# A batch's pp·w1 from eight fp32 products in 64x32 tiles, straight into its final layout, in place of split products through DRAM

## The chip, the cores and the metric

One core of one Trainium2 chip. The metric is device time in microseconds (us) of one launch; lower is better. The kernel before has a median of 977.68 us over three runs.

## The reference

For each of 8 batches: packed attention of 8 heads (32 packed rows `p` against 576 keys, then 576 queries `q` against the 32 packed rows), and a mixer on its result.

```python
p_packed = sm_attn(p, k, v)               # (8, 8, 32, 64): pp
out = sm_attn(q, p_packed, p_packed)      # a @ pp, a: (8, 8, 576, 32)
x = out.transpose(0, 2, 1, 3).reshape(B, S, H * D)     # (8, 576, 512)
h = x.transpose(0, 2, 1) @ U @ V
u = x + h.transpose(0, 2, 1)
ch = np.maximum(u @ w_ch1, 0.0) @ w_ch2   # w_ch1 (512, 2048), w_ch2 (2048, 512)
return u + ch
```

U, V, w_ch1 (w1) and w_ch2 (w2) arrive as float64; q, k, v, p as float32. Since x is a @ pp for each head, u @ w1 is (a plus its mixing) @ (pp·w1), where pp·w1 has 256 rows (8 heads of 32) and 2048 columns for each batch. This pp·w1 of a batch is what the change is about.

## The kernel before, in words

**The work.** The 2048 columns of w1 are done in two sweeps over all 8 batches, 1024 columns in each. A sweep has 8 steps `kt` of 128 columns for a batch. `gemm1(kt)` makes h from pp·w1 (tiles `wt`, hi and lo) and the attention weights (`ah`, `al`), 24 matmuls of 288 columns; ScalarE and VectorE take it out through relu as hi and lo; `gemm2(kt-1)`, one step behind, multiplies by w2 into four accumulators `o`, 12 matmuls of 512 columns (`joint` does the rest of the rows of two batches together). Every float32 product there is three products of float32r parts (`mm3`, lines 166 to 168: hi·hi, hi·lo, lo·hi). Sweep 0 stores `o` as `sum`, sweep 1 adds it.

**Around it, in sweep 0.** The attention of later batches runs in between: `packs` (keys, values and p of batch b+2), `attention` and `mixing` (queries of batch b+1). Float64 weights are made float32 by `convert`: a load of `bits` on SP's queue (two ahead), a ScalarE Abs (L228), four VectorE instructions (L229, L230, L234, L235), then a split into hi (ScalarE, L297) and lo (GpSimd, L298). What sweep 0 needs of w1 (8 items) and of w2 (8) is converted at the start, in one chain of 16; what sweep 1 needs of w2 in batches 2 and 3, of w1 in batches 5 and 6.

**pp·w1 before.** `fold(r, parts)` does it for two batches at once. pp is split into `lwh`, `lwl` (block diagonal), and for each 512 columns `c` and pair of heads `pr` an `mm3` with w1's hi and lo goes to one PSUM bank (68 in all, 204 matmuls), ScalarE copies it to an `ev` tile (L598, 3 of them, shared with the stores of `o` and of w2), and SP stores it to `wsb` in DRAM (L600). `load_wt` brings 256 columns back in the layout that gemm1 wants (L615, one `raw` tile), `split_wt` makes hi (ScalarE, L620) and lo (GpSimd, L621). This goes on 64 times, two pieces ahead.

**What sets the order.** All engines run fixed programs. The order is set while the program is written by a planner, `Chains`: each piece of side work is a generator with a due time, its needs (`banks`, `take`) and the flags that it comes after; `place()` puts ready pieces in between the products, and `until(...)` places nothing but side work till something is done. Times in `step(...)` are the planner's estimates. An engine that waits in its program holds all that stands behind it, and SP's queue, which issues every DMA, does so too. The first gemm1 stands behind `until("attention0", "fold0_0", "w2_0")`, the third step of batch 0 behind `until("fold0_1")`, which needs the packs of batch 1. Six PSUM banks serve the side work before the first gemm1 and two (`psT`) after it.

## Time and profile before

| | us |
|---|---|
| runs | 977.68, 978.88, 975.24 |
| median | 977.68 |
| profiled execution, its own time | 974.02 |
| its span in the trace | 972.3 |
| TensorE's mean granted clock in it, as a share of 2.4 GHz | 0.925 |

Section 1 of the page gives busy times by engine: TensorE 851.4 us (88%), VectorE 412.9, ScalarE 367.6, GpSimd 198.0. TensorE's busy time counts a matmul from its start to its modelled end, so where matmuls follow one another closely their starts tell how long one takes. A granted clock of 1.00 is 2.4 GHz, of 0.50 is 1.2 GHz; a stretch in between had some of each. In rows of waits, "A <- B" means that A stood still until B was done.

### The profile page before, as it was taken

The numbers are of one execution on the slowest core, as the hardware profiler recorded it, in microseconds if no ns is written. First come the engines' busy times: TensorE is split into PE (matmuls) and PEld (weight loads), VectorE is DVE, ScalarE is ACT, GpSimd is POOL, SyncE is SP. The second block draws the span as 40 slices with busy tenths as digits, with TensorE's granted clock in tenths as the row PEclk, the third lists the DMA queues.
The fourth block names the chain that finished last, engine by engine and source line by source line (L and its number), as shares of the span: only waits on it lengthen the run. The fifth ranks groups of instructions, "written<-read, shape, count | busy, mean of one in ns | idle before, by whom it ended". The sixth has DMA issues, their size and how long they took to land.

```text
span 972.3 us, 15520 instructions
## 1 busy us (share of the span) xinstructions
PE 851.4 (88%) x5452; PEld 703.8 (72%) x5452; DVE 412.9 (42%) x1122; ACT 367.6 (38%) x1065; POOL 198.0 (20%) x193
## 2 busy tenths in 40 slices
PE   4563697888999839999987999999999999999997
PEld 2342375666678628688766878888888888898996
DVE  2663556433556624444477722314131332423232
ACT  3542454343455424445544452334333322322220
POOL 0223223111233212212234411111111111111110
PEclk9665788798999979999998999999999999999999
DMA  7535554254547652623555162674353524324131
GB/s 218 161 86 172 176 158 130 98 155 117 182 153 243 210 173 73 201 90 123 155 158 179 55 179 93 245 227 149 117 165 112 190 66 139 115 83 160 42 109 66
DMA packets 101917, 139.06 MB, mean 143 GB/s; under 512 B 18896, under 2 KB 67408, under 8 KB 101840
## 3 DMA queue, kind: packets, MB, share of 16 engines
q1 hardware_dynamic: 101840, 138.07, 45.8%
q8 instruction: 44, 0.72, 0.3%
q14 instruction: 33, 0.27, 0.1%
HBM read 87.62 MB, written 50.41 MB: 142 GB/s over the span
## 4 chain that ended last, share of the span: by engine, by line
PE 71%; DMA 9%; DVE 8%; ACT 4%; POOL 3%; issue 3%; SPq 1%; DVEq 0%; ACTq 0%; POOLq 0%
PE o L166 13%; PE o L167 13%; PE o L168 13%; PE h_ps L166 7%; PE h_ps L168 6%; PE h_ps L167 6%; DMA xt<-in_k_dram 3%; PE t_ps L378 2%; PE t_ps L167 2%; PE t_ps L395 2%; PE t_ps L168 2%; PE t_ps L166 1%; DMA wsb<-ev 1%; PE t_ps L405 1%; DVE ts L229 1%
## 5 line engine op out<-in xcount | busy, mean ns | idle before, releaser
L712 DVE SCALAR_TENSOR_TENSOR hl<-h_ps,hh 128x256 fp32r<-128x256 f32 x256 | 107.7, 421 | 326.8 <-ACT hjh L710 325.8
L166 PE MATMUL o<-w2h,hh 128*128 128x512 f32 x512 | 209.4, 409 | 8.7 <-DVE ev L734 3.8
L167 PE MATMUL o<-w2l,hh 128*128 128x512 f32 x512 | 202.7, 396 | 3.5 <-POOL w2l L298 3.5
L168 PE MATMUL o<-w2h,hl 128*128 128x512 f32 x512 | 202.6, 396 | 0.0
L710 ACT ACTIVATE hh<-h_ps 128x256 fp32r<-128x256 f32 x256 | 98.4, 386 | 265.5 <-PE h_ps L168 265.3
L166 PE MATMUL h_ps<-ah,wth 128*128 128x288 f32 x512 | 159.2, 311 | 17.1 <-ACT wth L620 13.6
L621 POOL TENSOR_TENSOR wtl<-raw,wth 128x512 fp32r<-128x512 f32 x64 | 83.8, 1310 | 428.2 <-ACT wth L620 415.9
L168 PE MATMUL h_ps<-ah,wtl 128*128 128x288 f32 x512 | 154.2, 301 | 1.2 <-POOL wtl L621 1.2
L167 PE MATMUL h_ps<-al,wth 128*128 128x288 f32 x512 | 154.0, 301 | 0.0
L166 PEld LDWEIGHTS h_ps<-ah,wth 128*128 128x128 f32 x512 | 99.4, 194 | 31.0 <-ACT wth L620 13.8
L166 PEld LDWEIGHTS o<-w2h,hh 128*128 128x128 f32 x512 | 97.3, 190 | 30.5 <-DVE ev L734 5.2
L168 PEld LDWEIGHTS o<-w2h,hl 128*128 128x128 f32 x512 | 97.2, 190 | 21.0
L167 PEld LDWEIGHTS o<-w2l,hh 128*128 128x128 f32 x512 | 97.5, 190 | 17.4 <-POOL w2l L298 4.1
L167 PEld LDWEIGHTS h_ps<-al,wth 128*128 128x128 f32 x512 | 99.6, 194 | 4.0
L168 PEld LDWEIGHTS h_ps<-ah,wtl 128*128 128x128 f32 x512 | 99.1, 194 | 1.8 <-POOL wtl L621 1.8
L598 ACT COPY ev<-t_ps 128x512 f32<-128x512 f32 x68 | 39.9, 586 | 105.5 <-PE t_ps L168 77.8
L166 PE MATMUL t_ps<-w1h,lwh 128*128 128x512 f32 x68 | 32.5, 478 | 33.6 <-ACT ev L598 17.2
L378 PE MATMUL t_ps<-ident,xt 128*128 128x128 f32 x256 | 44.5, 311 | 9.7 <-DVE aT L551 3.2
L379 ACT COPY xT<-t_ps 128x512 f32<-128x512 f32 x64 | 37.6, 590 | 36.6 <-PE t_ps L378 36.5
L710 ACT ACTIVATE hjh<-h_ps 128x32 fp32r<-128x32 f32 x256 | 50.1, 196 | 0.0
L378 PEld LDWEIGHTS t_ps<-ident,xt 128*128 128x128 f32 x256 | 36.1, 161 | 18.4 <-DVE aT L551 3.5
L229 DVE TENSOR_SCALAR ts<-ts 128x512 f32<-128x512 f32 x32 | 31.0, 970 | 37.9 <-ACT ts L228 37.7
(130 smaller groups left out, 1165.3 us busy)
## 6 DMA issues: line engine op xcount, KB each, us to landing
bits<-in_moe_w_ch_dram SPq DMA_DIRECT2D x32, 512.0 KB, 4.1
wsb<-ev SPq DMA_DIRECT2D x128, 128.0 KB, 2.4
raw<-wsb SPq DMA_DIRECT2D x64, 256.0 KB, 2.7
xt<-in_k_dram SPq DMA_DIRECT2D x16, 512.0 KB, 4.7
xt<-in_v_dram SPq DMA_DIRECT2D x16, 512.0 KB, 4.7
xt<-in_q_dram SPq DMA_DIRECT2D x16, 512.0 KB, 4.2
sum<-ev SPq DMA_DIRECT2D x32, 256.0 KB, 2.2
part<-sum SPq DMA_DIRECT2D x32, 256.0 KB, 4.6
```

What stands on the lines that cost most here:

```text
L166: nc.tensor.matmul(ps, lhsT=lh, rhs=rh, start=start, stop=False)
L167: nc.tensor.matmul(ps, lhsT=lh, rhs=rl, start=False, stop=False)
L168: nc.tensor.matmul(ps, lhsT=ll, rhs=rh, start=False, stop=stop)
L229: nc.vector.tensor_single_scalar(t, t, LEAST, op=ALU.max)
L378: nc.tensor.transpose(t_ps[:, P * a:P * a + P], pairs[:, P * c:P * c + P], ident)
L379: nc.scalar.copy(t[:, 2 * h2:2 * h2 + 2, HT:HS], t_ps.rearrange("p (h x) -> p h x", h=2))
L395: nc.tensor.matmul(ss[r][hs, :HS], lhsT=lT[rs, g, hs], rhs=t[rs, h, HT * (1 - r):HT * (1 - r) + HS], start=True, stop=True)
L405: nc.tensor.transpose(t_ps[:, o:o + P], src[:, BLOCK[kk]:BLOCK[kk] + P], ident)
L598: nc.scalar.copy(st, w_ps)
L621: nc.gpsimd.tensor_tensor(lo, raw, hi.bitcast(F32), op=ALU.subtract)
L710: nc.scalar.activation(hi, src, AF.Relu)
L712: nc.vector.scalar_tensor_tensor(lo, src, 0.0, hi.bitcast(F32), op0=ALU.max, op1=ALU.subtract)
```

## The change

For each sweep, batch and 512 columns `fold` is now a chain of its own, 32 in all. It multiplies pp by w1 with eight plain fp32 matmuls of 512 columns, each in a tile of 64 rows by 32 columns of the array (a pair of head and column group by one of two row groups), into two PSUM banks, in the layout that gemm1 reads. From there ScalarE copies hi and VectorE subtracts lo into `wt`, of which there are two of 512 columns. Nothing goes to DRAM. w1 is kept as float32 (in 3 slots of 512 columns for each of four tiles), so that its conversion ends with VectorE's last instruction; a w1 item is loaded with two DMAs of 64 rows. Each fold may start when its batch's packs are done, w1's four items for its columns are there and a `wt` is free, that is, when gemm1 has ended with the piece before the last. Step 0 and step 4 of each batch stand behind `until` for their fold. The first chain of conversions no longer comes after the loads of batch 0's keys and values, and its first two items are loaded on ScalarE's DMA queue; w1's second half is converted in two chains of four, in batches 6 and 7. `pn` has two buffers and is loaded ahead of its turn, x tiles go from 6 to 7, pp goes to DRAM once for each batch and comes back for all batches at the start of sweep 1.

```diff
-    QW = 256
+    QW = 512
     NPC = NKS * P // QW
...
-    NX = 6
+    NX = 7
...
-    wsb = {(b, c): dram.tile([H * NP, 512], F32, name=f"wsb{b}_{c}", tag=f"wsb{b}_{c}")
-           for b in range(B) for c in range(4)}
...
-    side = Chains(6, xt=NX, xT=2, e=3, eT=2, pT=1, aT0=1, aT1=1)
+    side = Chains(6, xt=NX, xT=2, e=3, eT=2, pT=1, ppT=4, aT0=1, aT1=1, wt=2)
...
-    def float32_2(x, raw):
+    def float32_2(x, raw, out):
         low, high = raw[:, :, 0], raw[:, :, 1]
         nc.vector.scalar_tensor_tensor(x, high, -0x40000000, x, op0=ALU.bitwise_and, op1=ALU.bitwise_or)
-        nc.vector.scalar_tensor_tensor(x, low, 29, x, op0=ALU.logical_shift_right, op1=ALU.bitwise_or)
-        return x.bitcast(F32)
+        nc.vector.scalar_tensor_tensor(out.bitcast(I32), low, 29, x, op0=ALU.logical_shift_right, op1=ALU.bitwise_or)
...
-    def w1_slices(pr, c):
-        cs = slice(512 * (c % 2), 512 * (c % 2) + 512)
-        return tuple(t[:, cs] for t in w1t[pr])
-
-    def parts_w1(pr, c):
-        return w1[pr * P:(pr + 1) * P, 1024 * c:1024 * c + 1024], lambda: w1_slices(pr, c), None
+    def w1_slice(x, c):
+        return w1t[x][:, 512 * (c % 3):512 * (c % 3) + 512]
+
+    def parts_w1(x, c):
+        rows = [w1[256 * g + 64 * x:256 * g + 64 * x + 64, 1024 * c:1024 * c + 1024] for g in range(2)]
+        return rows, w1_slice(x, c), None
...
+    def load_bits(srcs, queue=None):
         bits = bits_tile()
-        nc.sync.dma_start(out=bits.rearrange("p x t -> p (x t)"), in_=src)
+        n = P // len(srcs)
+        for i, src in enumerate(srcs):
+            (queue or nc.sync).dma_start(out=bits[n * i:n * i + n].rearrange("p x t -> p (x t)"), in_=src)
...
         for i, (name, due, (_, parts, after)) in enumerate(items):
-            x = float32_2(xi, bits.pop(i))
+            split = callable(parts)
+            float32_2(xi, bits.pop(i), xi if split else parts)
             load(i + 2)
             yield step(0, ("DVE", 1.4))
-            hi, lo = parts()
-            nc.scalar.copy(hi, x)
-            nc.gpsimd.tensor_tensor(lo, x, hi.bitcast(F32), op=ALU.subtract)
-            if after:
-                after((hi, lo))
+            if split:
+                hi, lo = parts()
+                x = xi.bitcast(F32)
+                nc.scalar.copy(hi, x)
+                nc.gpsimd.tensor_tensor(lo, x, hi.bitcast(F32), op=ALU.subtract)
+                if after:
+                    after((hi, lo))
+                side.spend(0, [("ACT", 0.62), ("POOL", 1.3)])
             side.flags.add(name)
-            side.spend(0, [("ACT", 0.62), ("POOL", 1.3)])
...
-        pn = s1.tile([P, 2, 2, D], F32, name="pn", bufs=1)
+        pn = s1.tile([P, 2, 2, D], F32, name="pn", bufs=2)
-        yield step(0, ("DMA", 0.3), need=1)
+        yield step(0, ("DMA", 0.8), need=1, take=("pT",))
+        packed[b] = packed.get(b, 0) + 1
+        if packed[b] == 2 and b not in kept:
+            kept.add(b)
-        nc.sync.dma_start(out=ppTd[b][:, P * g:P * g + P], in_=ppT[b][:, g])
+            nc.sync.dma_start(out=ppTd[b], in_=ppT[b].rearrange("p g n -> p (g n)"))
...
-    lwh, lwl = (pipe.tile([P, 4, P], F32R, name=f"lw{x}", tag=f"lw{x}") for x in "hl")
-    for t in (lwh, lwl):
-        nc.gpsimd.memset(t.bitcast(F32), 0.0)
-    def fold(r, parts, fresh=(0, 1)):
...
-        for i, (c, batches) in enumerate(parts):
-            for pr in range(4):
-                w_ps = bank()
-                mm3(w_ps, (lwh[:, pr], lwl[:, pr]), w1_slices(pr, c), True, True)
-                st = out_tile()
-                nc.scalar.copy(st, w_ps)
-                for b2 in batches:
-                    nc.sync.dma_start(out=wsb[2 * r + b2, c][64 * pr:64 * pr + 64], in_=st[64 * b2:64 * b2 + 64])
...
-    pieces = [(sw, b, c) for sw in range(2) for b in range(B) for c in range(NPC)]
-    raws, wt = {}, {}
-
-    def load_wt(i):
-        sw, b, c = pieces[i]
-        raws[i] = pipe.tile([P, 2, QW], F32, name="raw", bufs=1)
-        cc = c * QW
-        src = wsb[b, 2 * sw + cc // 512][:, cc % 512:cc % 512 + QW]
-        nc.sync.dma_start(out=raws[i], in_=src.rearrange("(g m) x -> m g x", g=2))
-
-    def split_wt(i):
-        raw = raws.pop(i)
-        hi, lo = (pipe.tile([P, 2, QW], F32R, name=f"wt{x}", tag=f"wt{x}", bufs=2) for x in "hl")
-        nc.scalar.copy(hi, raw)
-        nc.gpsimd.tensor_tensor(lo, raw, hi.bitcast(F32), op=ALU.subtract)
-        wt[i] = hi, lo
+    wt = {}
+
+    def fold(sw, b, c):
+
+        f_ps = [bank() for _ in range(2)]
+        for x in range(4):
+            xs = slice(32 * x, 32 * x + 32)
+            for g in range(2):
+                gs = slice(64 * g, 64 * g + 64)
+                nc.tensor.matmul(f_ps[g][xs], lhsT=ppT[b][gs, g, xs], rhs=w1_slice(x, 2 * sw + c)[gs], start=True, stop=True)
+        hi, lo = wt[sw, b, c] = tuple(pipe.tile([P, 2, QW], F32R, name=f"wt{x}", tag=f"wt{x}", bufs=2) for x in "hl")
+        for g in range(2):
+            nc.scalar.copy(hi[:, g], f_ps[g])
+            nc.vector.tensor_tensor(lo[:, g], f_ps[g], hi[:, g].bitcast(F32), op=ALU.subtract)
+        if (sw, c) == (0, 1):
+            side.give("ppT")
+        yield step(1.2, ("ACT", 0.59), ("DVE", 0.69), ("DVE", 0.69))
...
+    def add_fold(sw, b, c):
+        after = [f"w1_{x}_{2 * sw + c}" for x in range(4)]
+        after += [f"packs{b}{g}" for g in range(2)] if sw == 0 else ["ppT"]
+        n = (sw * B + b) * NPC + c - 1
+        if n >= 0:
+            after.append(f"fold{n // (B * NPC)}{n // NPC % B}{n % NPC}")
+        side.add(f"fold{sw}{b}{c}", line(sw, b, 4 * c) - 1, fold(sw, b, c), after, need=2, take=("wt",))
...
-    items = [(f"w1_{pr}_0", -4 + pr / 4, parts_w1(pr, 0)) for pr in range(4)] + [("w2_0", -2, parts_w2(0))]
-    items += [(f"w1_{pr}_1", line(0, 0, 1) + pr / 4, parts_w1(pr, 1)) for pr in range(2)]
-    items += [("w2_1", line(0, 0, 1.5), parts_w2(1))]
-    items += [(f"w1_{pr}_1", line(0, 0, 1) + pr / 4, parts_w1(pr, 1)) for pr in range(2, 4)]
-    items += [(f"w2_{kt}", line(0, 0, kt) - 0.5, parts_w2(kt)) for kt in range(2, NKS)]
-    side.add("convert", -4.5, convert(items), after=("packs01l",))
+    items = [(f"w1_{x}_0", -4 + x / 4, parts_w1(x, 0)) for x in range(4)] + [("w2_0", -2, parts_w2(0))]
+    items += [("w2_1", line(0, 0, 1) - 0.5, parts_w2(1))]
+    items += [(f"w1_{x}_1", line(0, 0, 1) + x / 4, parts_w1(x, 1)) for x in range(2)]
+    items += [("w2_2", line(0, 0, 2) - 0.5, parts_w2(2))]
+    items += [(f"w1_{x}_1", line(0, 0, 2) + x / 4, parts_w1(x, 1)) for x in range(2, 4)]
+    items += [(f"w2_{kt}", line(0, 0, kt) - 0.5, parts_w2(kt)) for kt in range(3, NKS)]
+    side.add("convert", -4.5, convert(items, nc.scalar))
...
-    side.add("fold0a", -3, fold(0, [(0, (0,))], (0,)), ("packs00", "packs01"))
     add_packs(1)
-    side.add("fold0", line(0, 0, 2), fold(0, [(1, (0, 1)), (0, (1,))], (1,)), ("packs10", "packs11", "fold0a"))
-    side.until("attention0", "fold0_0", "w2_0")
-    for i in range(2):
-        load_wt(i)
-        split_wt(i)
...
             self.h[kt] = hh, hl
+            if kq == QW // P - 1:
+                side.give("wt")
 
         def gemm2(self, kt):
             if kt == self.kts[0]:
...
-    for r in range(1, B // 2):
-        side.add(f"fold{r}", line(0, 2 * r - 1, 3), fold(r, [(0, (0, 1)), (1, (0, 1))]),
-                 (*(f"packs{2 * r + i}{g}" for i in range(2) for g in range(2)), f"fold{r - 1}"))
-    items = [(f"w1_{pr}_{c}", line(0, 6, 0) + 4 * c - 8 + pr, parts_w1(pr, c)) for c in (2, 3) for pr in range(4)]
-    side.add("convert_w1", line(0, 6, 0), convert(items), (f"fold{B // 2 - 1}", "convert_w2"))
-    side.add("again0", line(0, 7, 4), fold(0, [(2, (0, 1)), (3, (0, 1))]), ("convert_w1",))
+    for sw in range(2):
+        for b in range(B):
+            for c in range(NPC):
+                if (sw, b, c) != (0, 0, 0):
+                    add_fold(sw, b, c)
     items = [(f"w2_{kt}", line(0, 3, kt), parts_w2_later(kt)) for kt in range(NKS, NK)]
     side.add("convert_w2", line(0, 3, 0), convert(items), ("attention2", "convert"))
+    for c in range(2, 4):
+        items = [(f"w1_{x}_{c}", line(0, B - 2, 8 * (c - 2)) + 2 * x, parts_w1(x, c)) for x in range(4)]
+        side.add(f"convert_w1{c}", items[0][1], convert(items), ("convert_w2",) if c == 2 else ("convert_w12", f"fold0{B - 1}0"))
...
-            for r in range(1, B // 2):
-                side.add(f"again{r}", line(1, 2 * r - 1, 3), fold(r, [(2, (0, 1)), (3, (0, 1))]), (f"again{r - 1}",) if r > 1 else ())
+            for b in range(B):
+                ppT[b] = pool.tile([P, 2, P], F32, name=f"ppT{b}", tag=f"ppT{b}")
+                nc.sync.dma_start(out=ppT[b].rearrange("p g n -> p (g n)"), in_=ppTd[b])
+            side.flags.add("ppT")
         for b in range(B):
...
-                if (sw, b) == (0, 0) and j == 2:
-                    side.until("fold0_1")
-                    load_wt(2)
-                if sw == 0 and b % 2 == 1 and j == 4 and b + 1 < B:
-                    side.until(f"fold{(b + 1) // 2}")
-                if (sw, b, j) == (0, B - 1, 4):
-                    side.until("again0")
-                if sw == 1 and b % 2 == 1 and j == 4 and b + 1 < B:
-                    side.until(f"again{(b + 1) // 2}")
+                if j % (QW // P) == 0:
+                    side.until(f"fold{sw}{b}{j * P // QW}")
```

## Rows read from the trace of the kernel before

**Rows 1.** Page, section 1: busy us of each engine, share of the span, instructions

```profile
PE 851.4 (88%) x5452; PEld 703.8 (72%) x5452; DVE 412.9 (42%) x1122; ACT 367.6 (38%) x1065; POOL 198.0 (20%) x193
```

**Rows 2.** Stages: stretch, its us, busy (x) PE PEld DVE ACT POOL, clock, DMA, GB/s

```profile
0.00:84.90 84.90, 39.63 (x374) 27.42 (x374) 42.80 (x98) 34.01 (x79) 18.42 (x26) 0.71 0.54 157
84.90:126.90 42.00, 27.16 (x112) 18.53 (x113) 21.53 (x44) 16.28 (x37) 11.25 (x9) 0.62 0.54 163
126.90:193.50 66.60, 57.72 (x422) 45.16 (x420) 37.89 (x87) 29.54 (x80) 18.02 (x18) 0.85 0.44 135
...
325.80:401.30 75.50, 59.08 (x373) 44.51 (x374) 33.20 (x89) 31.14 (x86) 17.10 (x16) 0.89 0.48 146
401.30:461.20 59.90, 58.88 (x508) 47.30 (x507) 27.52 (x85) 27.33 (x81) 13.49 (x15) 1.00 0.39 125
461.20:518.60 57.40, 49.88 (x325) 41.58 (x325) 33.74 (x77) 28.64 (x77) 19.07 (x17) 0.91 0.52 153
...
615.80:972.30 356.50, 349.34 (x1959) 308.54 (x1958) 103.45 (x350) 102.95 (x353) 40.02 (x31) 1.00 0.42 134
```

**Rows 3.** TensorE's waits, 0 to 85, 200 to 300, 300 to 400: us, times, longest

```profile
PE h_ps L166 <- ACT wth L620: 13.6, 1, 13.6
PE t_ps L166 <- ACT w1h L297: 9.5, 3, 4.8
...
PE t_ps L166 <- ACT ev L598: 7.1, 1, 7.1
...
PE t_ps L166 <- ACT ev L598: 10.1, 2, 9.2
```

**Rows 4.** Order of time, SP and ScalarE, opening: start us, us, engine, line, operation

```profile
18.62 0.91 SPq L269 DMA_DIRECT2D bits<-in_moe_w_ch_dram  x2
...
30.44 0.62 ACT L297 CAST w1h<-wd 128x512 fp32r<-128x512 f32 x1
...
78.09 8.53 SPq L615 DMA_DIRECT2D raw<-wsb  x2
...
100.71 0.62 ACT L297 CAST w1h<-wd 128x512 fp32r<-128x512 f32 x1
...
121.77 0.61 ACT L297 CAST w1h<-wd 128x512 fp32r<-128x512 f32 x1
...
178.04 0.62 ACT L297 CAST w2h<-wd 128x512 fp32r<-128x512 f32 x1
...
193.47 1.08 ACT L736 COPY ev<-o 128x512 f32<-128x512 f32 x2
```

**Rows 5.** Waits of SP's queue over the whole span: us, times, longest

```profile
SPq L615 <- POOL wtl L621: 194.7, 48, 10.0
```

**Rows 6.** Order of time, TensorE, around one set of scores in sweep 0

```profile
415.93 0.39 PE L167 MATMUL o<-w2l,hh 128*128 128x512 f32 x1
416.16 0.40 PE L168 MATMUL o<-w2h,hl 128*128 128x512 f32 x1
...
416.93 0.29 PE L167 MATMUL h_ps<-al,wth 128*128 128x288 f32 x1
417.06 0.29 PE L168 MATMUL h_ps<-ah,wtl 128*128 128x288 f32 x1
417.28 0.72 PE L395 MATMUL t_ps<-xT,pT 64*32 64x288 f32 x16
...
418.17 0.29 PE L167 MATMUL h_ps<-al,wth 128*128 128x288 f32 x1
```

**Rows 7.** Groups by line and shape: busy us, mean ns | idle before, releasers

```profile
L598 ACT COPY ev<-t_ps 128x512 f32<-128x512 f32 x68 | 39.9, 586 | 105.5 <-PE t_ps L168 77.8 <-DMA wsb<-ev 18.9 <-issue 2.9
L166 PE MATMUL t_ps<-w1h,lwh 128*128 128x512 f32 x68 | 32.5, 478 | 33.6 <-ACT ev L598 17.2 <-ACT w1h L297 13.2 <-DVE e L500 2.3
L530 DVE TENSOR_TENSOR tl<-t_ps,th 128x512 fp32r<-128x512 f32 x16 | 11.0, 688 | 13.3 <-ACT th L529 13.3
```

**Rows 8.** Order of time, SP's queue, ahead of 222 us

```profile
218.04 8.49 SPq L600 DMA_DIRECT2D wsb<-ev  x13
```

More of the change, by code (lines that the diff above doesn't have):

```diff
@@ L230, in float32_1 @@
         nc.vector.tensor_scalar(x, t.bitcast(I32), 3, 0x3FFFFFF8, op0=ALU.logical_shift_left, op1=ALU.bitwise_and)
[L232 removed]
+    def float32_2(x, raw, out):
         low, high = raw[:, :, 0], raw[:, :, 1]
         nc.vector.scalar_tensor_tensor(x, high, -0x40000000, x, op0=ALU.bitwise_and, op1=ALU.bitwise_or)
[L235 to L236 removed]
+        nc.vector.scalar_tensor_tensor(out.bitcast(I32), low, 29, x, op0=ALU.logical_shift_right, op1=ALU.bitwise_or)
     def float32_of(x, t, raw):
         float32_1(x, t, raw)
[L240 to L243 removed]
+        float32_2(x, raw, x)
+        return x.bitcast(F32)
+    w1t = [pipe.tile([P, 3 * 512], F32, name=f"w1t{i}", tag=f"w1t{i}") for i in range(4)]
     w2t = {}
@@ L264, in keep, with convert @@
                 nc.sync.dma_start(out=w2d[kt, x], in_=t.bitcast(F32))
-        return w2[kt * P:(kt + 1) * P, :], lambda: [out_tile(F32R) for _ in "hl"], keep
-    def load_bits(src):
+        return [w2[kt * P:(kt + 1) * P, :]], lambda: [out_tile(F32R) for _ in "hl"], keep
+    def load_bits(srcs, queue=None):
         bits = bits_tile()
-        nc.sync.dma_start(out=bits.rearrange("p x t -> p (x t)"), in_=src)
+        n = P // len(srcs)
+        for i, src in enumerate(srcs):
+            (queue or nc.sync).dma_start(out=bits[n * i:n * i + n].rearrange("p x t -> p (x t)"), in_=src)
         return bits
-    def convert(items):
+    def convert(items, queue=None):
         n = len(items)
@@ L278, in load @@
             if i < n:
-                bits[i] = load_bits(items[i][2][0])
+                bits[i] = load_bits(items[i][2][0], queue if i < 2 else None)
                 side.spend(0, [("DMA", 1.9)])
@@ L629, in add_packs @@
     def add_packs(b):
-        free = ((f"attention{b - 3}",) if b > 2 else ()) + ((f"fold{b // 2 - 2}",) if b > 3 else ())
-        side.add(f"pT{b}", line(0, b - 2, b % 2), turn_p(b), free, take=("pT",))
+        free = (f"attention{b - 3}",) if b > 2 else ()
+        side.add(f"pT{b}", line(0, b - 2, b % 2), turn_p(b), free + (f"pT{b - 1}",), take=("ppT",))
         for g in range(2):
```

38 lines of the change are left out of this document (6 added, 32 removed).

## The prediction

> **What bounds the kernel now.** I read the busy times by engine first. TensorE leads with 851.4 of 972.3 us and no other engine passes 413 [rows 1], so the kernel is TensorE's unless it stands still or runs slow. The table of stages comes next, since such a mean hides both. From 615.8 on (sweep 1) TensorE is busy 349.3 of 356.5 us at clock 1.00: there only its own work counts. A batch of sweep 0 with attention and joint can be as dense: 401.3 to 461.2 took 59.9 us, 58.9 of them busy, at clock 1.00. The rest of sweep 0 falls short of that: the opening up to 84.9 has 39.6 us busy at clock 0.71, the next 42.0 us have 27.2 at 0.62, and the batch from 325.8 took 75.5 us at 0.89 [rows 2].
>
> Third, what ended TensorE's idle time. Before the first gemm1 it stood 13.6 us for `wth`, the reloaded pp·w1; in the opening 9.5 us for w1's hi parts; later 7.1 and 10.1 us for `ev`, the fold's way out [rows 3]. The order of time says why. At 78.09 SP issues the two `raw` loads and spends 8.53 us on them, since the second waits for the only `raw` tile [rows 4]; before 222 it issues 13 `wsb` stores, over 8.49 us, which had stood behind loads in its queue [rows 8]. Over the span SP's queue waits 194.7 us for `wtl` ahead of `raw` loads, and loads of keys, queries and weights stand behind that [rows 5]. The path through DRAM thus costs at two places: in its own chain, and in the queue that feeds everything else.
>
> **Prices.** One product of 512 columns takes 0.23 us (415.93 to 416.16), one of 288 columns 0.13 [rows 6]. The change takes away 204 of the former, 204 x 0.23 = 46.9 us at full clock. No row shows the new product with 512 columns; the nearest is a set of scores, also eight fp32 products in 64x32 tiles, with 288 columns. It stands between 417.06 + 0.13 = 417.19 and 418.17 - 0.13 = 418.04: 0.85 us [rows 6]. If all of that grows with the columns, 512 cost 1.51 us. The trace has 16 instructions for the eight products, two in succession in each tile; if each streams at twice the price of an h product, 4 x 0.13 = 0.52 us grow and 0.33 stay: 0.33 + 0.52 x 512/288 = 1.25. I take 1.25 because the eight overlap in the record (16 in 0.72 us), and keep 1.51. Then 32 folds cost 40 to 48 us against 46.9. TensorE's own work hardly changes; the change is about waits.
>
> Getting one fold out of PSUM: two ScalarE copies of 0.59 us (L598) and two VectorE subtractions of 0.69 (L530) [rows 7], some 0.59 + 0.69 + 0.69 = 2.0 us from the last product to the last lo. GpSimd loses all of `wtl`, ScalarE one copy of two. VectorE gains 64 x 0.69 = 44 us on 413, which is cover as long as no wait stands on it.
>
> **Term 1, opening and batch 0.** Now 193.5 us, up to the first store copy at 193.47 [rows 4]. Removed: the `raw` wait of 13.6 us at the first gemm1, of which attention 0 (its last store went out just before 78.09) leaves some 7; TensorE's standing in single fold products for single w1 items, 9.5 us; and the third step's wait for the other half of w1 and the packs of batch 1, most of the stage of 42.0 us for two of eight steps. What is late next? The conversions: sixteen must pass, and the last, at 178.04, stands 15.4 us before the batch's end [rows 4]. They keep a pace of 7.0 us at best over some intervals (100.71 to 121.77, three) and of 9.8 over all (30.44 to 178.04, fifteen). In the change the first loads no longer stand behind the keys and the rest of SP's queue (18.62 us), and a conversion takes 11.8 us from issue to its first cast, so the sixteenth comes at 12 + 15 x 8 = 132 at a pace of 8, and the batch ends at 147. At 7.0 it is 132, and that is about what TensorE needs too, 60 us [rows 2] after a first gemm1 at some 72 (84.9 less the 7 and about half of the 9.5); at 9.8 it is 174. I take 147, between them, because SP no longer blocks but ScalarE and VectorE remain shared: 46 us gained, bounds 20 and 61. The two loads on ScalarE's queue cost it an issue each (SP spends 0.91 us on two [rows 4]), at a time when it has little to do.
>
> **Term 2, later stalls of the fold.** 7.1 and 10.1 us [rows 3] go, as `ev` and `wsb` go from this chain, and some slow clock: the stages around them had 0.89 [rows 2], 75.5 x 0.11 = 8 us at most, part of it idle anyway. I take 20, bounds 12 and 28. Late next there is VectorE, whose conversions of w2 run in the same batches.
>
> **Term 3, w1's second half.** Four of its eight conversions move from batches 5 and 6 into batch 7, which has no attention. The stage from 461.2 had VectorE busy 33.7 of 57.4 us and TensorE idle 7.5 [rows 2]. I take 6, bounds 0 and 10.
>
> **Term 4, TensorE's own work.** In sweep 0, batches 1 to 7, 96 products x 0.23 = 22 us become 14 folds x 1.25 = 17.5: 4.5 gained. In sweep 1, 96 less the 24 of `again0`, so 72 x 0.23 = 16.6 us, become 16 x 1.25 = 20, and the first fold there stands alone, as its flag is set only when the sweep starts: some 2 us of evacuation in the open. That is 5.4 lost, in a stage that hides nothing. I take 0 in all, bounds 4 gained and 6 lost (at 1.51).
>
> **Term 5, new waits.** `fold` takes both side banks for its product and its evacuation, 1.25 + 2.0 us, 32 times, and attention waits with its transposes meanwhile. Main products are placed between, so most is covered; I take 4 lost, bounds 0 and 12. Coming in halves, w1's 16 loads are 16 more issues on SP's queue, against 128 `wsb` and 64 `raw` ones less: no cost.
>
> **The sum** against the profiled execution's own 974.0: -46 - 20 - 6 + 0 + 4 = -68, which is 906. The median of the runs is 3.7 above that execution; I leave the number.
>
> **The rivals.** *Conversions still pace the opening.* At 9.8 us term 1 gives 20: 974 - 20 - 20 - 6 + 4 = 932. For it: the slow pace over fifteen intervals. Against it: its slow stretches hold SP's and the fold's waits. 18%.
>
> *Evacuation comes into the open (slower).* If each fold is made so late that gemm1 waits for it, TensorE stands for the chain of 2.0 us and some 0.6 of handovers between the engines (an estimate), 2.6 us, in each of 32: 906 + 83 = 989. It turns the sign from 68/32 = 2.1 us a fold. For it: `until` at steps 0 and 4 places no products. Against it: `wt` has two buffers, so a fold has four steps, some 15 us in sweep 1 (a third of 356.5/8 = 44.6), to get done. 4%. The Trainium skill, TensorEngine Tiling (Array Packing), section PSUM Bottleneck, says that tiling speeds up TensorE but not the way out of PSUM, which may become the bottleneck; by it the change would come out at this rival's 989, and the rows agree with its premise (2.0 us out against 1.25 in), not with its being exposed.
>
> *The eight products run one after another.* Then a fold is 16 instructions of two 0.23 passes, 7.4 us: 906 + 32 x 6.1 = 1101. Against it: the scores' 16 in 0.72 us [rows 6]. 2%.
>
> *Another chain paces sweep 0 anyway* (VectorE, 37.9 of 66.6 us in batch 0 already [rows 2], with more to do): about 974, 4%.
>
> **How the numbers follow.** The forecast, 876 to 925, has 67%; better than that 5%; the first rival 18%, the others 10%. The range takes in the first rival with some room and not every bound at once (those add up to 871 and 961): 876 to 950. A measurement of this kernel can tell about 0.5% from no change; faster by more has 90%, within it 4%, slower 6%.
>
> **What would show it.** Right: the first gemm1 near 72, batch 0 ending near 147, no TensorE wait of several us before `t_ps` outside the opening, batch 3 (now 75.5) near 63, sweep 1 some 5 us longer, and fold products 1.25 us apart from their neighbours. Wrong: conversions that keep a pace near 10 us, TensorE waiting before h products for the fold's hi or lo at every fourth step, or fold products that don't overlap.

## The result and the profile after

The changed kernel takes 931.08 us (median of 4 runs, 926.49 to 931.87) against 977.67 (4 runs, 975.24 to 978.88): a ratio of 0.9517, 95% interval 0.9481 to 0.9552. It is faster and inside the range of 876 to 950, but 25 us short of the 906 that was forecast and outside the 876 to 925 that had 67%. The gain is 47 us where 68 were expected. The profiled execution took 931.87 with a span of 930.0; that of before 974.0 with 972.3.

Busy times by engine, after ([rows 1] has those before):

```profile
PE 839.7 (90%) x5760; PEld 668.7 (72%) x5760; DVE 432.5 (47%) x1154; ACT 313.2 (34%) x949; POOL 93.9 (10%) x111
```

TensorE lost 12 of 851 busy us, GpSimd half of its work, and VectorE gained 20 on 413. What moved the end is not seen here but by stage. A stage of the fence ends where ScalarE makes its first copy of a batch's output (columns as in [rows 2]): opening, batches 0 to 7, sweep 1.

```profile
0.00:69.70 69.70, 37.24 (x379) 23.65 (x379) 38.16 (x97) 28.53 (x70) 9.80 (x17) 0.76 0.58 155
69.70:168.30 98.60, 76.41 (x500) 54.93 (x500) 58.67 (x134) 37.63 (x101) 20.95 (x21) 0.77 0.49 148
168.30:227.10 58.80, 54.83 (x434) 41.52 (x433) 26.94 (x74) 23.48 (x70) 8.21 (x10) 0.94 0.34 104
227.10:293.10 66.00, 60.21 (x469) 47.12 (x468) 43.83 (x105) 30.17 (x86) 14.79 (x15) 0.95 0.59 191
293.10:358.50 65.40, 57.30 (x443) 43.22 (x441) 35.48 (x90) 28.17 (x79) 12.26 (x13) 0.95 0.47 143
358.50:416.80 58.30, 57.38 (x469) 45.71 (x468) 30.99 (x88) 24.86 (x75) 8.70 (x10) 1.00 0.37 118
416.80:485.20 68.40, 60.15 (x444) 45.85 (x443) 34.05 (x87) 25.80 (x73) 8.39 (x10) 0.88 0.18 60
485.20:535.20 50.00, 47.56 (x295) 37.57 (x294) 30.35 (x70) 17.78 (x54) 10.77 (x16) 0.97 0.29 93
535.20:574.20 39.00, 37.55 (x225) 31.12 (x224) 15.28 (x45) 11.25 (x40) 0.00 (x0) 1.00 0.25 85
574.20:930.00 355.80, 351.12 (x2117) 297.98 (x2115) 118.74 (x368) 85.52 (x315) 0.00 (x0) 1.00 0.27 93
```

| stage | before, us | after, us | difference | forecast |
|---|---|---|---|---|
| up to the first gemm1 | 84.9 | 69.7 | -15.2 | -13 |
| batch 0 | 108.6 | 98.6 | -10.0 | -33 |
| batches 1 to 4 | 267.7 | 248.5 | -19.2 | -20 (term 2) |
| batches 5 to 7 | 153.2 | 157.4 | +4.2 | -6 (term 3) |
| sweep 1 | 357.9 | 355.8 | -2.1 | +5.4 (of term 4) |

Two of the rows before, with the same edges, from which batch 0 and sweep 1 are read:

```profile
84.90:193.50 108.60, 84.88 (x533) 63.70 (x533) 59.42 (x131) 45.81 (x117) 29.27 (x27) 0.76 0.48 146
...
614.40:972.30 357.90, 350.74 (x1966) 309.69 (x1964) 104.50 (x352) 103.54 (x354) 40.02 (x31) 1.00 0.42 133
```

The differences add up to the 42.3 us between the two profiled spans. Two stages missed: batch 0 by 23 us and batches 5 to 7 by 10. Sweep 1 gave 7.5 us more than forecast. The forecast's remaining terms (4.5 off in sweep 0, 4 on for new waits) have no stage of their own. The stages also do not hold the same side work. Of the 16 packings (`packs`, one for each half of a batch's heads, 40 products at L474, before L470) two lie in batch 0 where three did, and two in batch 5 where one did, so part of what batch 0 gave came back as work in batch 5.

TensorE's longest waits after, over the whole span (line waited at, what ended the wait: us in total, times, longest):

```profile
PE t_ps L386 <- ACT xT L383: 12.7, 2, 12.2
PE t_ps L425 <- DMA pn<-in_p_dram: 9.5, 3, 5.2
PE t_ps L409 <- ACT e L450: 9.2, 8, 2.9
...
PE t_ps L399 <- DVE wtl L593: 4.3, 3, 1.5
```

The waits of [rows 3] for `wth`, w1's hi parts and `ev` are gone. One of 12.2 us is new. In order of time (SPq is SP's queue; start us, us; for several in succession xcount; in brackets the idle time before and what ended it):

```profile
83.10 0.38 SPq L357 DMA_DIRECT2D xt<-in_k_dram  x1
...
90.99 0.98 SPq L371 DMA_DIRECT2D xt<-in_v_dram  x2
92.52 1.57 SPq L270 DMA_DIRECT2D bits<-in_moe_w_ch_dram  x3
99.53 0.66 ACT L227 ACTIVATE ts<-bits 128x512 f32<-128x512 f32 x1 [12.18 <-DMA bits<-in_moe_w_ch_dram]
100.09 0.58 ACT L383 COPY xT<-t_ps 128x512 f32<-128x512 f32 x1
100.72 0.48 PE L386 MATMUL t_ps<-ident,xt 128*128 128x128 f32 x1 [12.20 <-ACT xT L383]
```

Read it from the bottom. TensorE waits for a copy on ScalarE (L383). That copy stands behind a conversion (L227), which waits for its `bits`. The load of those bits was issued at 92.52, behind 9 us of key and value loads in SP's queue. Only the first two items, four loads, go through ScalarE's queue; the other 20 loads of the first chain still go through SP. In this batch the clock is 0.77.

### The profile page after: what moved, and what is told of

The parts are those of the page before. It is cut to its first block, busy times and chain, and to the rows that moved or that the text cites. A ratio compares the mean times of both kernels' runs of the same rounds, so it can differ in the third digit from the quotient of the medians.

```text
span 930.0 us, 15444 instructions
## 1 busy us (share of the span) xinstructions
PE 839.7 (90%) x5760; PEld 668.7 (72%) x5760; DVE 432.5 (47%) x1154; ACT 313.2 (34%) x949; POOL 93.9 (10%) x111
## 4 chain that ended last, share of the span: by engine, by line
PE 80%; DMA 7%; DVE 6%; ACT 3%; issue 2%; SPq 1%; POOL 0%; ACTq 0%; DVEq 0%
PE o L168 16%; PE o L169 15%; PE o L170 15%; PE h_ps L168 7%; PE h_ps L169 7%; PE h_ps L170 7%; PE t_ps L589 4%; PE t_ps L382 3%; DMA bits<-in_moe_w_ch_dram 2%; PE t_ps L399 2%; PE t_ps L409 2%; PE t_ps L543 1%; DMA sum<-ev 1%; PE t_ps L474 1%; DMA xt<-in_v_dram 1%
## 5 line engine op out<-in xcount | busy, mean ns | idle before, releaser
L168 PE MATMUL o<-w2h,hh 128*128 128x512 f32 x512 | 212.9, 416 | 3.3 <-DVE ev L715 2.5
L169 PE MATMUL o<-w2l,hh 128*128 128x512 f32 x512 | 203.2, 397 | 1.4 <-POOL w2l L302 1.4
L170 PE MATMUL o<-w2h,hl 128*128 128x512 f32 x512 | 202.8, 396 | 0.0
L169 PE MATMUL h_ps<-al,wth 128*128 128x288 f32 x512 | 155.8, 304 | 0.3
L170 PE MATMUL h_ps<-ah,wtl 128*128 128x288 f32 x512 | 155.2, 303 | 0.0
L170 PEld LDWEIGHTS o<-w2h,hl 128*128 128x128 f32 x512 | 97.5, 190 | 21.4
L169 PEld LDWEIGHTS o<-w2l,hh 128*128 128x128 f32 x512 | 97.7, 191 | 14.9 <-POOL w2l L302 2.2
L169 PEld LDWEIGHTS h_ps<-al,wth 128*128 128x128 f32 x512 | 100.2, 196 | 5.0 <-POOL al L563 1.4
L170 PEld LDWEIGHTS h_ps<-ah,wtl 128*128 128x128 f32 x512 | 100.4, 196 | 0.0
L593 DVE TENSOR_TENSOR wtl<-t_ps,wth 128x512 fp32r<-128x512 f32 x64 | 41.2, 686 | 49.8 <-ACT wth L592 49.7
L592 ACT CAST wth<-t_ps 128x512 fp32r<-128x512 f32 x64 | 34.4, 589 | 51.6 <-PE t_ps L589 51.6
L383 ACT COPY xT<-t_ps 128x512 f32<-128x512 f32 x64 | 37.1, 588 | 41.4 <-PE t_ps L382 41.2
L691 DVE SCALAR_TENSOR_TENSOR hjl<-h_ps,hjh 128x32 fp32r<-128x32 f32 x256 | 46.2, 181 | 0.0
L589 PE MATMUL t_ps<-w1t,ppT 64*32 64x512 f32 x512 | 39.1, 644 | 3.6 <-DVE xT L389 1.5
```

What stands on the lines that cost most here:

```text
L168: nc.tensor.matmul(ps, lhsT=lh, rhs=rh, start=start, stop=False)
L169: nc.tensor.matmul(ps, lhsT=lh, rhs=rl, start=False, stop=False)
L170: nc.tensor.matmul(ps, lhsT=ll, rhs=rh, start=False, stop=stop)
L383: nc.scalar.copy(t[:, 2 * h2:2 * h2 + 2, HT:HS], t_ps.rearrange("p (h x) -> p h x", h=2))
L589: nc.tensor.matmul(f_ps[g][xs], lhsT=ppT[b][gs, g, xs], rhs=w1_slice(x, 2 * sw + c)[gs], start=True, stop=True)
L592: nc.scalar.copy(hi[:, g], f_ps[g])
```

## Experiments

Each kernel is the changed one with the edit shown, unless it says "from the kernel before". Behind a measured median stand, in brackets, its ratio to the kernel before and the 95% interval of that ratio. Experiments 6 and 8 have two executions each, the others four or more. "Last conversion" is the end of the sixteenth conversion of the first chain, "end of batch 0" the copy as above. The changed kernel has 154.6 and 168.3.

**1. The early start, taken back.** All loads of the first chain on SP, and the chain behind the second packing, as before the change.

```diff
-    side.add("convert", -4.5, convert(items, nc.scalar))
+    side.add("convert", -4.5, convert(items), after=("packs01l",))
```

> The changed kernel with one part undone: the first chain's loads are back on SP's queue and come after the loads of batch 0's keys and values, as before the change. In my prediction this part was worth up to 18 us, as it lets the conversions start earlier. The trace speaks against it: the first w1 conversion ends at 32.5 with the change and 29.7 without. Theory (that step of term 1 was wrong, an earlier load gives nothing as long as ScalarE and VectorE do the packs first): 931 within 4 us. Rival (it is worth what I put on it): 940 to 949.

Measured: 925.61 (0.9480, 0.9445 to 0.9514), within the interval of the changed kernel or slightly better. The first conversion ends at 31.3 instead of 32.5, the last at 152.5, batch 0 at 166.2. The early start brings nothing. The trace of the changed kernel shows why:

```profile
0.73 2.49 ACTq L270 DMA_DIRECT2D bits<-in_moe_w_ch_dram  x4
...
28.96 0.67 ACT L227 ACTIVATE ts<-bits 128x512 f32<-128x512 f32 x1
```

The loads go out at 0.73 and land at most 8.7 us after their issue, but the first conversion's first step (L227) runs at 28.96. The due time of the chain, -4.5, places it behind packs, q0, scores and `uv` (-9.5 to -4.8).

**2. Due times of the first five conversions moved ahead.**

```diff
-    items = [(f"w1_{x}_0", -4 + x / 4, parts_w1(x, 0)) for x in range(4)] + [("w2_0", -2, parts_w2(0))]
+    items = [(f"w1_{x}_0", -10 + x / 4, parts_w1(x, 0)) for x in range(4)] + [("w2_0", -9, parts_w2(0))]
```

(and the chain itself from -4.5 to -10.5)

> The changed kernel with one edit: the planner's due times of the first chain's first five conversions are moved ahead of those of batch 0's packs (-10 to -9 in place of -4 to -2), so that they also stand ahead of the packs in ScalarE's and VectorE's programs. My term 1 had the sixteenth conversion at 12 + 15 x 8 = 132; in the changed kernel the first one ended at 32.5 and the last at 154.6, a pace of 8.1, so what failed was the 12, some 20 us. Theory (batch 0's end hangs on the chain of conversions, and this on when its first one is done): the first ends near 12 to 15, the last 15 to 20 us earlier, batch 0 ends 12 to 20 us earlier, 911 to 919. Rival (the packs and attention 0 then stand behind the conversions and come as much later, since VectorE does both): first gemm1 later by 8 to 13 us, 925 to 940.

Measured: 935.29 (0.9563, 0.9530 to 0.9595), no gain. The first conversion now ends at 10.9 and the fifth at 47.2 (63.2 in the changed kernel), but the sixth only at 76.6 (71.5) and the last at 157.9. Batch 0 ends at 171.6. So the conversions are not one chain that an early start shifts as a whole: five belong to the opening, eleven are due after the first step.

**3. The other loads of the first chain on GpSimd's queue,** and **on ScalarE's.**

```diff
-                bits[i] = load_bits(items[i][2][0], queue if i < 2 else None)
+                bits[i] = load_bits(items[i][2][0], queue)
-    side.add("convert", -4.5, convert(items, nc.scalar))
+    side.add("convert", -4.5, convert(items, nc.gpsimd))
```

(for ScalarE the first pair of lines alone)

> As a1, but the first chain's loads are on GpSimd's DMA queue, whose engine is busy for only 10% of the span. Theory (SP's queue): about 911 again, or a little less, since ScalarE issues nothing and waits for no buffer. Rival (pace of VectorE and ScalarE): 927 or more. A difference of over 4 us between a1 and a2 would be the price of issuing from ScalarE.

> The changed kernel with one edit: all 16 items of the first chain of conversions are loaded on ScalarE's DMA queue, not the first two alone. In the changed kernel TensorE stands still for 12.2 us at 88 to 100, because ScalarE's Abs waits for a bits load that SP issued at 92.5, behind four loads of keys and values; the clock is at half for most of 91 to 132 after it. Theory (batch 0 lost its expected gain to SP's queue): the stall goes and the clock stays up, some 12 + 8 = 20 us, so about 911. Rival (the conversions' pace is that of VectorE and ScalarE, the stall only shows it): under 4 us, so 927 or more. Should ScalarE's own waits for a free bits buffer cost as much as SP's did, it is no faster either, and the trace shows ScalarE's queue waiting ahead of those issues.

Measured: on GpSimd's queue 916.48 (0.9379, 0.9346 to 0.9411), the fastest kernel here, 14.6 us ahead of the changed one. On ScalarE's 928.5 (0.9512, 0.9482 to 0.9542), no difference that can be told. The stage of batch 0 with GpSimd's queue:

```profile
70.80:159.40 88.60, 74.15 (x500) 53.82 (x501) 58.28 (x136) 38.67 (x103) 28.35 (x33) 0.84 0.58 165
```

The same 500 matmul instructions take 10 us less, the clock is 0.84 instead of 0.77, and TensorE's longest wait there is 2.5 us in total (L169 for `w2l`). On ScalarE's queue the 12.2 us wait is gone as well, but the opening is 6.3 us longer (the first gemm1 comes at 76.0), and in batch 0 TensorE waits 4.0 us for `w2h` and 3.9 us for `xT`, both ScalarE's. Of the 12.7 us between the profiled executions of the changed kernel and of GpSimd's queue, 8.9 lie before the end of batch 0 and the rest behind it, where nothing was edited.

The blocking in SP's queue went both ways. In the changed kernel, from 60 to 180, the longest sum of SP's own waits is that of the weight loads for a `bits` tile that a conversion (L234) has not yet read:

```profile
SPq L270 <- DVE wd L234: 28.9, 5, 8.2
```

The key, query and value loads stand behind these waits, as the weight load at 92.52 stands behind them. With GpSimd's queue neither holds the other; which of the two gives the 8.9 us is not shown apart.

**4. Both: late start, and early due times, each with all loads on GpSimd's queue.** The edits are those of 1 and 2 joined with 3.

> The first chain starts behind the second packing as it did before the change (no early start), with all its loads on GpSimd's queue. Theory: the early start gives nothing (the first chain on SP behind the second packing was 925.6, against 931.1), and the 12.2 us stall is that of SP's queue alone, so this is as the loads on GpSimd's queue with the early start or up to 5 us faster: 911 to 917, batch 0's end at 155 to 160. Rival: the early start is what gives time once the loads don't queue behind the x loads; then 921 to 926, batch 0's end near 166 as it was with the late start on SP.

> The early due times of a7 together with the first chain's loads on GpSimd's queue (a2, which measured 916.5 against 931.1 of the changed kernel). If the two causes are separate, their gains add: 897 to 905. If they are the same wait twice (both only bring the conversions forward), it is within 4 us of the better of the two.

Measured: 918.74 (0.9415, 0.9388 to 0.9441) and 917.23 (0.9371, 0.9335 to 0.9408), neither to be told from 916.48. When the first five conversions run makes no difference, on either queue.

In all the kernels up to here batch 0 ends 13.7 us after the last conversion: 154.6 and 168.3 (changed), 152.5 and 166.2 (1), 157.9 and 171.6 (2), 145.7 and 159.4 (3, GpSimd), 158.0 and 171.7 (3, ScalarE), 142.9 and 156.6, 142.8 and 156.5 (4). And from the sixth to the sixteenth conversion the pace is 8.0 to 8.3 us with loads on SP's or ScalarE's queue, 7.2 on GpSimd's. So in these kernels the end of batch 0 goes with the last conversion, and the pace goes with the queue of the loads. The whole follows only roughly: what comes behind batch 0 took between 754.1 and 762.0 us in these seven profiled executions.

**5. The eleven later conversions let go earlier,** with the loads on GpSimd's queue.

```diff
+    items = [(n, min(d, -2 + 0.01 * i), parts) for i, (n, d, parts) in enumerate(items)]
```

> All sixteen loads of the first conversion chain on GpSimd's queue, and besides the eleven conversions after the first five get due times ahead of the planner's horizon (-2 + 0.01 i), so that they may run before the first step instead of one by one after it. Theory: with the loads out of SP's queue, the end of batch 0 hangs on these eleven, which the planner holds until the first step is on its way, one per 7 to 8 us; let go earlier, some of them end before the first gemm1 (more than the five or six of now), which stays within 3 us of 70.8, the last one ends near 132 instead of 145.7, batch 0 near 147 instead of 159.4, and the time is about 905 (loads alone on that queue: 916.5). Rival: VectorE and ScalarE are full in the opening, so each conversion made earlier moves the first attention and the first gemm1 back by as much; first gemm1 after 80, batch 0's end 157 or later, and the time is 914 or more.

Measured: 934.34 (0.9559, 0.9538 to 0.9581): 18 us worse than the same loads without it. The expectation of 905 fell. First gemm1 is at 71.3, so the opening was not too full, which the rival had assumed. Yet the last conversion ends at 154.8, and batch 0 at 177.7, 22.9 us later instead of 13.7. SP's queue, in order of time and its longest wait from 60 to 180:

```profile
103.75 0.98 SPq L371 DMA_DIRECT2D xt<-in_v_dram  x2
146.59 0.35 SPq L487 DMA_DIRECT2D ppTd<-ppT  x1
147.03 0.39 SPq L357 DMA_DIRECT2D xt<-in_q_dram  x1
```

```profile
SPq L487 <- ACT ppT L482: 41.7, 1, 41.7
```

SP stands 41.7 us at the store of a packed p, whose last copy on ScalarE comes that late, and the query loads are behind it. With the loads alone on GpSimd's queue the same wait is 36.7 us in two pieces. So the stand is only 5 us longer in all. That the conversions put ahead delayed the packing fits the order of time, but it was not tried by itself (the store on another queue was not run), and what cost the 18 us stays open.

**6. One buffer for the folded weights instead of two.**

```diff
-    side = Chains(6, xt=NX, xT=2, e=3, eT=2, pT=1, ppT=4, aT0=1, aT1=1, wt=2)
+    side = Chains(6, xt=NX, xT=2, e=3, eT=2, pT=1, ppT=4, aT0=1, aT1=1, wt=1)
```

(and the tiles `wth`, `wtl` with one buffer)

> One buffer for the folded weights instead of two, so that no fold can be made before the last gemm1 of the quarter ahead of it has read its weights, and ScalarE's and VectorE's evacuation lies between two steps. Theory: with two buffers the evacuation (2.0 us) is hidden everywhere, and uncovered it costs 2.0 to 2.6 us a fold: sweep 1 is 16 x 2.0 to 2.6 = 32 to 42 us longer (388 to 398 instead of 355.8), and the whole is 990 to 1015. Rival: work of gemm2 and of other chains covers it even so, and sweep 1 is less than 15 us longer; or it was already in the open, and nothing changes (within 5 us of 931).

Measured: 918.45 (0.9405, 0.9383 to 0.9427), 12.6 us *faster* than with two. The theory fell. The rival was right on sweep 1 (less than 15 us longer), but that the whole gets faster was not foreseen. Batch 5 and sweep 1:

```profile
417.70:471.00 53.30, 50.28 (x351) 38.98 (x350) 31.48 (x79) 21.24 (x61) 7.95 (x9) 0.97 0.23 77
559.50:916.70 357.20, 352.44 (x2134) 297.97 (x2132) 119.96 (x370) 86.65 (x317) 0.00 (x0) 1.00 0.27 92
```

Sweep 1 is 1.4 us longer than with two, and 17 more instructions on TensorE, about one fold, fall into it. The evacuation costs nothing even so. The order of time shows the cover:

```profile
577.85 1.09 PE L589 MATMUL t_ps<-w1t,ppT 64*32 64x512 f32 x16
578.87 0.50 PE L168 MATMUL o<-w2h,hh 128*128 128x512 f32 x1
579.03 1.07 ACT L592 CAST wth<-t_ps 128x512 fp32r<-128x512 f32 x2 [1.29 <-PE t_ps L589]
579.65 1.29 DVE L593 TENSOR_TENSOR wtl<-t_ps,wth 128x512 fp32r<-128x512 f32 x2 [1.35 <-ACT wth L592]
...
583.94 0.29 PE L168 MATMUL h_ps<-ah,wth 128*128 128x288 f32 x1
```

The last lo is done at 579.65 + 1.29 = 580.94; the first h product with it comes at 583.94, and TensorE has gemm2 products until then, and from 581.06 on the 24 residual products of sweep 1 (`add_u`). Batch 5 took 68.4 us with two buffers and 53.3 with one. With two, three folds lie in it (436.9, 452.3, 460.1), both of batch 6 among them; with one, two (433.1, 455.1). The changed kernel, end of batch 5:

```profile
461.92 1.29 DVE L593 TENSOR_TENSOR wtl<-t_ps,wth 128x512 fp32r<-128x512 f32 x2 [1.35 <-ACT wth L592]
463.12 0.74 DVE L517 TENSOR_REDUCE s<-e 128x18 f32<-128x576 f32 x1
...
464.96 1.52 DVE L234 SCALAR_TENSOR_TENSOR w1t<-bits,wd 128x512 int32<-128x512 int32 x1
466.40 0.77 DVE L523 STREAM_TRANSPOSE aT<-e 128x576 f32<-128x576 f32 x1
467.22 1.75 PE L409 MATMUL t_ps<-ident,aT 128*128 128x128 f32 x7 [3.62 <-DVE aT L523]
```

VectorE stands 1.35 us for a fold that is first needed in the middle of batch 6 and works on it for 1.29; then come the softmax of the next attention and a conversion; TensorE waits 3.62 us for `aT`. Behind that wait the granted clock is at the lower of its two levels (columns as above):

```profile
470.00:480.00 10.00, 8.43 (x30) 6.93 (x30) 3.33 (x9) 3.06 (x9) 3.07 (x4) 0.50 0.19 75
```

So more is lost here than the 3.6 us themselves. The whole stage stands at 0.88, with one buffer at 0.97.

The two stages do not hold the same work: 444 TensorE instructions in batch 5 with two buffers, 351 with one. With one buffer a fold and a packing fewer lie there, and batch 3 has the packing (120 products at L474 in place of 80). The end of batch 4 is no later for it (417.7, against 416.8), and batches 5 to 7 together take 141.8 us against 157.4. The edit changed the planner's order of all this side work, so the folds, the packing and the clock are not told apart.

**7. The fold's way out by ScalarE and GpSimd** (two copies to `ev` on ScalarE, the hi from there, the lo on GpSimd), which takes VectorE out.

```diff
+        raw = [out_tile() for g in range(2)]
         for g in range(2):
-            nc.scalar.copy(hi[:, g], f_ps[g])
-            nc.vector.tensor_tensor(lo[:, g], f_ps[g], hi[:, g].bitcast(F32), op=ALU.subtract)
+            nc.scalar.copy(raw[g], f_ps[g])
+        for g in range(2):
+            nc.scalar.copy(hi[:, g], raw[g])
+            nc.gpsimd.tensor_tensor(lo[:, g], raw[g], hi[:, g].bitcast(F32), op=ALU.subtract)
```

> The changed kernel with one edit in how a fold leaves PSUM: ScalarE alone copies both banks to two ev tiles, and then hi is a ScalarE copy from there and lo a GpSimd subtraction, in place of hi and VectorE's lo straight from the banks. VectorE loses 64 x 0.69 = 44 us, ScalarE gains 64 x 0.6 = 38 us, GpSimd 64 x 1.3 = 84 us, and the banks are free about 0.7 us sooner. Theory (my term 5, the 44 us on VectorE and the held banks cost some 4 us; waits of 1.4 us of the next user of a bank for wtl stand four times in the trace, 6 us): 4 to 8 us faster, 923 to 927. Rival (the ev tiles, shared with the stores, bring the waits of the kernel before back): slower, 935 or more, with waits for ev ahead of t_ps in the trace.

Measured: 945.4 (0.9684, 0.9653 to 0.9714), 14 us slower. The rival came: TensorE waits for `ev` ahead of `t_ps` (L399, 2.2 us, 3 times). Sweep 1 is again 355.8, so there the way out is free by either engine; sweep 0 pays, where the longer way makes TensorE wait for the lo (L170 for `wtl`, 3.7 us, 6 times) and ScalarE's 346 busy us instead of 313 fall. These two waits are 5.9 of the 14 us; the rest stays open.

**8. The eight products of each fold issued twice.**

```diff
-        for x in range(4):
+        for x in (*range(4), *range(4)):
```

> The eight products of each fold are issued twice, the second time over the first, so the result is the same and only TensorE's work grows. Theory: each set costs about 1.0 us of TensorE's time at full clock (the insertion was 1.22 us, with 0.2 of it the change-over), all of it on the path in sweep 1, where TensorE is nearly always busy: sweep 1 is 16 us longer (372). In sweep 0 TensorE's waits swallow part of it: 0 to 22 us more. The whole is 947 to 969. Rival: the fold's products fill waits of TensorE everywhere and cost nothing: within 5 us of 931.

Measured: 949.73 (0.9725, 0.9692 to 0.9758), 18.7 us more. Sweep 1:

```profile
578.40:945.90 367.50, 362.77 (x2341) 302.17 (x2340) 118.63 (x368) 85.57 (x315) 0.00 (x0) 1.00 0.27 90
```

It is 11.7 us longer with 2341 - 2117 = 224 more instructions, that is 14 sets of 16: 0.84 us a set, all on the path. (Fourteen, not sixteen: the first two folds of sweep 1 are made before this stage begins, in the changed kernel at 567.4 and 570.0.)

**9. From the kernel before: `raw` loads on GpSimd's queue; and with the `wsb` stores on ScalarE's besides.**

```diff
-        nc.sync.dma_start(out=raws[i], in_=src.rearrange("(g m) x -> m g x", g=2))
+        nc.gpsimd.dma_start(out=raws[i], in_=src.rearrange("(g m) x -> m g x", g=2))
```

> The kernel before with one edit: the 64 raw loads (L615) are issued on GpSimd's queue, right behind the wtl that frees their buffer, so that SP's queue no longer waits the 194.7 us for wtl. The way through DRAM stays. Theory A (what the change gains outside the opening is mostly SP's queue being free): 12 to 20 us faster, 955 to 965. Theory B (it gains by the round trip's own chain: the raw wait at the first gemm1, the wait for the other half of w1, the stores behind ev): 4 us or less, 970 to 980.

> The kernel before with two edits: raw loads on GpSimd's queue, as in b1_raw_pool (972.0), and the wsb stores on ScalarE's queue, right behind the copy that they wait for, so that no part of the way through DRAM stands in SP's queue any more. Theory (the later stalls of 7.1 and 10.1 us come from wsb stores that stand behind loads in SP's queue): both stalls go, with some slow clock behind them, 15 to 25 us less than b1_raw_pool, 947 to 957. Rival (128 issues on ScalarE, some 0.4 us each, stand before its copies out of PSUM and cost as much as they give): 965 or more. The opening stays as it was, batch 0 ending near 193 in both.

Measured: 972.03 (0.9953, 0.9938 to 0.9968), and 991.35 (1.0141, 1.0118 to 1.0165). In the first, SP's 194.7 us for `wtl` [rows 5] are gone, and TensorE's waits on the way through DRAM are what they were (17.2, 13.6 and 13.2 us before):

```profile
PE t_ps L166 <- ACT ev L598: 17.9, 3, 9.2
PE h_ps L166 <- ACT wth L620: 14.0, 1, 14.0
PE t_ps L166 <- ACT w1h L297: 13.2, 5, 4.8
```

In the second, the wait for `ev` breaks up into 17 of at most 2.7 us, 14.8 in all, and the 128 stores take ScalarE some 0.45 us each to issue. It is 19 us slower than the first; that the issues are the reason fits its rival, but was not shown apart (the stores on GpSimd's queue were not tried). The blocking of SP's queue by `raw` was worth 5 us. That is not yet the worth of a free queue: in the first of these kernels SP waits longer elsewhere, 80.2 us ahead of weight loads (L269) and 111.4 ahead of `wsb` stores (L600), where it waited 50.1 and 97.1 before.

## Why the prediction was right or wrong

**Sign, and what goes away.** Right. The three waits of [rows 3] went with the path through DRAM, and batches 1 to 4, where the 7.1 and 10.1 us lay, gave 19.2 against 20. Batch 3, called at 63 from 75.5, took 65.4 between the edges above (80.1 before). One sign did not hold: "no TensorE wait of several us before `t_ps` outside the opening", as the wait of 12.2 us lies in batch 0. The part of *What bounds the kernel now* that fell is the second place of the DRAM path, "the queue that feeds everything else": experiment 9 prices the `raw` loads' part of it at 5 us. That the gains of the opening and of batches 1 to 4 come from the path through DRAM is read from the waits that went. The seventh x tile, the second `pn` buffer and w1 without its split came in the same change and were not tried by themselves.

**Term 1 (46 forecast, 25 measured).** The step that failed is "the sixteenth at 12 + 15 x 8 = 132". The pace was right: (154.6 - 32.5) / 15 = 8.1. The tail was right: 13.7 against 15.4. The start was not. I let the conversions begin when their loads had landed, and did not weigh the chain's due time, -4.5, behind everything with -9.5 to -4.8; the first one ended at 32.5, 20 us after the 12. Experiments 1 and 2 show that the 12 would not have helped either: with the first at 10.9 the sixth came at 76.6, since the eleven later ones have due times after the first step. So the sum was the wrong shape, not only wrong in one value: what counts is the sixth conversion at some 70 to 77 us and ten more at 7 to 8. And "SP no longer blocks" was half true. SP's queue was now held by the key, query and value loads and by the weight loads waiting for `bits`, with 12.2 us of TensorE's time at one place; experiment 3 takes the weight loads out and gets 14.6 us, 8.9 of them by the end of batch 0. The result lies on the first rival's 932, and the conversions do set the end of batch 0, but not by that rival's mechanism: the pace was not 9.8. That the total came so near to 932 is chance. Batch 0's gain is also helped by the packing that left it, which the term did not count.

The Trainium skill, DMA: Bandwidth & Descriptors, section Issuing engines are not separate DMA queues, says that issuing from several engines saves only the time that the sequencer needs to issue. By it the move is worth at most SP's issues, an estimate of 10 us for 20 (three took 1.57 us at 92.52). The runs gave 14.6 us on one queue, 8.9 of them by the end of batch 0, and nothing to be told on the other. So the part up to there is within that estimate and the whole is not; what a load stands behind, and what then stands behind it, counts here besides the issuing itself.

**Term 3 (6 gained forecast, 4 lost).** The step that failed is "four of its eight conversions move from batches 5 and 6 into batch 7" (the section on the change has them in batches 6 and 7, which is wrong too). By their last instruction one lies in batch 4 (390.1), three lie in batch 5, two in batch 6 (526.6, 530.6) and only two in batch 7. Those of batches 5 and 7:

```profile
440.62 0.69 DVE L234 SCALAR_TENSOR_TENSOR w1t<-bits,wd 128x512 int32<-128x512 int32 x1
...
445.83 0.69 DVE L234 SCALAR_TENSOR_TENSOR w1t<-bits,wd 128x512 int32<-128x512 int32 x1
...
464.96 1.52 DVE L234 SCALAR_TENSOR_TENSOR w1t<-bits,wd 128x512 int32<-128x512 int32 x1
...
536.16 0.69 DVE L234 SCALAR_TENSOR_TENSOR w1t<-bits,wd 128x512 int32<-128x512 int32 x1
...
541.06 0.69 DVE L234 SCALAR_TENSOR_TENSOR w1t<-bits,wd 128x512 int32<-128x512 int32 x1
```

So batch 5 lost one conversion of four, and took in what the term put at nothing: three folds, whose way out takes VectorE 6 x 0.69 = 4.1 us, and one packing more. The packings' products in batch 5, before and after:

```profile
L470 PE MATMUL t_ps<-xt,eT 128*32 128x64 f32 (+1 forms) x40 | 1.0, 223 | 0.7 <-DVE eT L460 0.5 <-ACT xT L379 0.2
...
L474 PE MATMUL t_ps<-xt,eT 128*32 128x64 f32 (+1 forms) x80 | 1.9, 223 | 2.0 <-DVE eT L464 2.0
```

Batch 6 gave 9.3 us and batch 5 cost 11.0, of which 10.3 are busy time of TensorE (60.15, from 49.88). Experiment 6 shows that this loss goes with the second `wt` buffer, with which the planner puts both folds of batch 6 and the second packing into batch 5. Which of these makes it is not shown.

**Term 4.** The price was right. Between products before and after it, a fold takes (613.63 + 0.23 = 613.86 to 615.31 - 0.23 = 615.08) 1.22 us against 1.25:

```profile
613.63 0.40 PE L170 MATMUL o<-w2h,hl 128*128 128x512 f32 x1
613.95 1.09 PE L589 MATMUL t_ps<-w1t,ppT 64*32 64x512 f32 x16
...
615.31 0.40 PE L169 MATMUL o<-w2l,hh 128*128 128x512 f32 x1
```

The account of sweep 1 failed: not 16 folds lie in its stage but 14, 14 x 1.22 = 17.1 against 16.6, and TensorE's busy time there is indeed only 0.4 us up (351.12, from 350.74). Its idle time fell from 7.2 to 4.7, so the stage is 2.1 us shorter. The first fold did not stand in the open there: it is made in batch 7, which is 2.5 us longer than before and in which the second fold (569.97) waits 1.45 us for the first one's lo.

**Term 5 (4 lost).** Right in kind: TensorE waits for a fold's lo to free a bank three times before another chain's product (L399, 4.3 us) and once before the next fold (L589, 1.45). The one other way out that was tried did not give it back (experiment 7).

**The rival of the evacuation in the open** was put at 4% and fell twice over: with two buffers, and with one (experiment 6), where my own argument for the cover, two buffers, no longer holds. In the place shown there, what covers it is the gemm2 and residual work that follows the fold. Its 0.6 us of handovers came from no row; in the one place where a fold's way out stands in the open, between the folds of 567.43 and 569.97, the gaps between the engines' instructions are under 0.1 us each. The rule that I had set beside it (the Trainium skill, TensorEngine Tiling (Array Packing), section PSUM Bottleneck) is not borne out as a wait in sweep 1: 2.0 us out for 1.25 in, and sweep 1 at 355.8 by VectorE, 355.8 by GpSimd and 357.2 with one buffer. That the products would run one after another is excluded by 1.22, and that another chain paces sweep 0 to 974 by the result.

**Two of the sums** do not come out by their own figures, and neither moves the forecast: at 1.51 term 4 loses some 8.6 (1.0 gained in sweep 0, 9.6 lost in sweep 1), not 6, and the worst bounds as stated add up to 960, not 961.

**A version faster than both** is that of experiment 3 with GpSimd's queue, 916.48. With experiment 6 added it was not tried.
